# Two tiles' transposes and two long warm-up matmuls ahead of the first v matmul, and row blocks 0, 1 of v of three tiles ahead of blocks 2, 3

## The chip, the cores and the metric

The kernel runs on one core of a Trainium2 chip. A core has a matrix engine (TensorE, PE in the profile; its weight loads are PEld), a vector engine (VectorE, DVE), an engine for activations and copies (ScalarE, ACT), a general one (GpSimd, POOL) and one that issues most of the DMAs (SyncE, SP). They run side by side and wait for each other by semaphores. Matmuls read from the on-chip memory SBUF and write to banks of PSUM, a second on-chip memory; ACT and DVE read these banks.

The metric is the device time of one execution in microseconds (us). The profile shows one further execution, instruction by instruction; its times count from the span's start.

## The reference

The input x has 2048 rows (tokens) of 512 numbers in bf16. It is normalized and goes through two branches, whose outputs are added to x:

```python
xn = _layernorm(x, axis=-1)                       # 2048 x 512
# branch A: linear attention, 32 heads of 16
q, k, v = split(xn @ wqkv)                        # 512 -> 3 * 512
pq, pk = q @ w_phi, k @ w_phi                     # per head, 16 x 16
phi_q = concat(softmax(pq), softmax(-pq))         # 32 features a head; phi_k alike from pk
kv = einsum("bhsf,bhsd->bhfd", phi_k, v);  z = phi_k summed over s
o  = (phi_q @ kv) / (phi_q @ z + 1e-6)
A  = o @ wo
# branch B: gated unit, 1792 wide
B  = ((xn @ w_gate) * (xn @ w_up)) @ w_down
return x + A + B
```

## The kernel before

The tokens are cut into 16 tiles of 128 and the tiles into 4 groups of 4. A matmul contracts over the 128 partitions, so each product with xn needs xn transposed (the tile xnT: four blocks of 128 features, a token per column). A product over 512 features is four matmuls, one for each block, which add up in one PSUM bank; the helper proj (L234) issues them for the blocks that it is given.

The order of the instructions on each engine is the order in which the program writes them (the manual schedule of L98). An instruction whose input is not ready holds up all that stand behind it on its engine; only weight loads may run ahead of matmuls. Waits are set by what an instruction reads and writes.

**Loads.** SP issues tile 0 of x, tile 2 of x, then wv in two halves (blocks 0, 1 and blocks 2, 3; L84 and L85), then the first columns of the gate and up weights, and so on (L82 to L95). ACT issues tiles 1 and 3 of x (L102, L103).

**The first group.** For tiles 0 to 3 the kernel does not wait for the statistics of the normalization. DVE takes the sum of a row (sum_of, L373; for tile 1 ACT does, L376) and subtracts it from 512 times the row (sub_sum, L337), which gives the tile xn. PE transposes its four blocks (lt, L205) into a PSUM bank, and ACT copies them to xnT (L206). The scale 1/deviation comes in later, when v is copied out of PSUM (first_v_out: L361 on DVE for tiles 0 and 1, L363 on ACT for tiles 2 and 3), from statistics that DVE and POOL work out beside this (stats_of, scales_of).

**v of the first group** is done by first_v (L353): tiles 0 and 1 into two banks of their own (kvbank), tiles 2 and 3 into banks of the shared pool of six (ps_s, L143), which hands out banks in turn: first to the warm-up matmuls (L304), then to the transposes of tile 0 (two banks), tile 1, and on in the order of the program.

**Warm-up matmuls** (warm_up, L306) multiply constants into a bank that nobody reads: with the second argument left out they are 512 columns wide, with 1 they are 128 wide. Seven long ones and a short one stand at the start (L311, L312).

The order of PE around the change, before: seven long warm-up matmuls and a short one; transposes of tile 0; two short warm-up matmuls; block 0 of v of tile 0; transposes of tile 1; block 1 of v of tile 0; transposes of tile 2; blocks 2, 3 of v of tile 0; v of tile 1; transposes of tile 3; v of tile 2; v of tile 3; then the first units of the gated branch.

**The rest.** A unit of the gated branch (ffn, L265) is four gate matmuls (L274), four up matmuls (L278), a copy by ACT (L281) and a product by DVE (L282) for 128 of the 1792 columns and 512 tokens. Three units come first, then the product of wk and w_phi (fold, L217, matmuls at L225), then units mixed with k features, kv sums and, for tile 4 and later, v (vproj). Tiles 4 to 15 are normalized by ACT (L192) and transposed by a DMA (L194). After the last kv sum come attention (attend, L458) and the output matmuls (fin, L284: w_down at L290, wo at L293), whose result DVE adds to x and SP stores.

Of the kernel before, what the change touches and what calls it, by code (L numbers as in the profile page):

```python
# [21 lines left out]
def kernel(  # L22
# [19 lines left out]
    DC = D // P  # L42
# [102 lines left out]
    def bank(name, dt=F32, n=TT):  # L145
        return ps_s.tile([P, n], dt, name=name, tag="s")
# [55 lines left out]
    def lt(n, lo=0, hi=DC):  # L202
        tp = bank("tp", BF16).rearrange("p (c t) -> p c t", c=DC)
        for c in range(lo, hi):
            nc.tensor.transpose(out=tp[:, c, :], in_=xns[n][:, c * P:(c + 1) * P], identity=ident[:])  # L205
        nc.scalar.copy(out=xnT[:, lo:hi, n * P:(n + 1) * P], in_=tp[:, lo:hi, :])  # L206
# [27 lines left out]
    def proj(ps, n, w, js=range(DC)):  # L234
        for j in js:
            nc.tensor.matmul(ps, lhsT=xnT[:, j, n * P:(n + 1) * P], rhs=w[:, j, :],  # L236
                             start=(j == 0), stop=(j == DC - 1))
# [68 lines left out]
    def warm_up(k, reps=DC):  # L306
        for _ in range(k):
            nc.tensor.matmul(warm[:, 0:reps * P], lhsT=ones,
                             rhs=nc.const_aps.tensor(1.0, [P, reps * P], BF16), start=True, stop=True)

    warm_up(7)  # L311
    warm_up(1, 1)  # L312

    with tc.tile_pool(name="ps_k", bufs=1, space=PSUM) as ps_k:
        kvbank = [ps_k.tile([P, TT], F32, name=f"kv{b}") for b in range(2)]
# [20 lines left out]
        def sub_sum(n, tot, lo=0, hi=D):  # L336
            nc.vector.tensor_scalar(out=xns[n][:, lo:hi], in0=xall[:, n, lo:hi], scalar1=float(D), scalar2=tot[:],  # L337
                                    op0=ALU.mult, op1=ALU.subtract)
# [14 lines left out]
        def first_v(n, js):  # L353
            if n not in vps:
                vps[n] = kvbank[n][:] if n < 2 else bank("pv")
            proj(vps[n], n, wv, js)
# [22 lines left out]
        sub_sum(1, tots[1])  # L379
        lt(0, 0, 2)  # L380
        lt(0, 2, DC)
        warm_up(2, 1)
        first_v(0, (0,))
        lt(1)
        first_v(0, (1,))
        for n in (2, 3):
            sum_of(n)
            sub_sum(n, tots[n])
        lt(2)
        first_v(0, (2, 3))  # L390
        first_v(1, range(DC))
        lt(3)
        first_v(2, range(DC))
        for n in (2, 3, 0, 1):
            stats_of(n)
            scales_of(n, float(D))
# [125 lines left out]
```

## Time and profile before

| what | value |
|---|---|
| three runs | 220.89, 221.40, 223.25 us; median 221.4 |
| the profiled execution | 221.23 us |
| its span, first to last instruction | 219.5 us |
| mean granted TensorE clock | 0.999 |
| PE busy | 214.5 us (98%), 1292 matmuls and transposes |
| DVE, ACT, POOL busy | 141.0 (64%), 89.4 (41%), 74.1 us (34%) |
| PE's waits in the first 30 us | 1.3 us for wv (L236), 0.8 us at the start |

How to read the lines that follow in this document. A row of a timeline has the start in us, the time in us, the engine, the line of the program, the operation, what it writes<-reads, its shape, the number of instructions merged into it (x4), and in brackets how long its engine was idle before it and what ended that. Matmuls overlap in the pipeline, so a row's time is longer than what it adds: the distance from one start to the next counts. A row of the chain of waits has start, time and what the time was spent on. A row of the stretches has its bounds, its length, and then for each engine the busy time and the number of instructions in the order PE, PEld, DVE, ACT, POOL, followed by the granted clock, the share of the DMA engines and GB/s. A row of a source line gives the shortest, median and longest instruction in ns and the first and last start; below it stands the time from a DMA's issue to its landing. An engine with a q (SPq) is its queue, which only issues or waits.

### The profile page before, as it was taken

The page shows a single profiled execution, that of the slowest core. Times are in us where ns is not written, and L with a number is a line of the kernel's source. Part 1 is how long each engine was busy: PE and PEld are TensorE (multiplying, and loading weights), DVE is VectorE, ACT ScalarE, POOL GpSimd, SP SyncE. Part 2 cuts the span into 40 slices and gives each one's busy share as a digit, 9 for nine tenths or more (in the row PEclk, how much of TensorE's full clock was granted, in tenths as well). Part 3 has the DMA queues.
Part 4 walks back from the last instruction along what each step waited for, and adds up shares of the span by engine and source line. Part 5 has one row for each costly group of instructions (what it writes and reads, how often), then busy time and mean ns, then how long its engine had stood idle before and what let it go on. Part 6 is the DMA issues. An engine that isn't in the chain of part 4 may idle for free.

```text
span 219.5 us, 3489 instructions
## 1 busy us (share of the span) xinstructions
PE 214.5 (98%) x1292; PEld 102.8 (47%) x1292; DVE 141.0 (64%) x239; ACT 89.4 (41%) x159; POOL 74.1 (34%) x71
## 2 busy tenths in 40 slices
PE   6999999999999999999999999999999999999994
PEld 2444445454444444444544444444444444444443
DVE  5858866886598757667499773196655645454321
ACT  5546586459665875465434222141231322100000
POOL 2540853363348463636045433033023033000000
PEclk9999999999999999999999999999999999999999
DMA  5999996102202431202018445114451431512301
GB/s 176 283 293 371 375 242 93 42 0 51 48 0 49 50 75 21 48 3 48 1 30 98 92 106 115 47 24 96 96 75 24 96 72 27 97 48 72 74 25 48
DMA packets 48529, 19.91 MB, mean 91 GB/s; under 512 B 37504, under 2 KB 48512, under 8 KB 48512
## 3 DMA queue, kind: packets, MB, share of 16 engines
q1 hardware_dynamic: 48224, 19.42, 39.8%
q10 hardware_dynamic: 288, 0.26, 0.4%
q8 instruction: 10, 0.16, 0.3%
q14 instruction: 7, 0.06, 0.1%
HBM read 8.67 MB, written 2.10 MB: 49 GB/s over the span
## 4 chain that ended last, share of the span: by engine, by line
PE 96%; DMA 2%; SPq 0%; DVE 0%; issue 0%
PE g L274 22%; PE fin L290 22%; PE u L278 22%; PE fin L293 6%; PE k L236 6%; PE q L236 6%; PE pv L236 6%; DMA wv<-in_A_wqkv_dram 2%; PE kv L330 2%; PE ab L461 2%; PE kv L236 1%; PE pq L225 1%; SPq L69 0%; PE tp L205 0%; DVE o_sb L300 0%
## 5 line engine op out<-in xcount | busy, mean ns | idle before, releaser
L274 PE MATMUL g<-xnT,wg 128*128 128x512 bf16 x224 | 57.5, 379 | 0.0
L278 PE MATMUL u<-xnT,wu 128*128 128x512 bf16 x224 | 57.5, 379 | 0.0
L282 DVE TENSOR_TENSOR hT<-u,g_sb 128x512 bf16<-128x512 f32 x56 | 37.0, 666 | 24.9 <-PE u L278 16.8
L253 POOL TENSOR_TENSOR phiq<-e,rsum 128x1024 bf16<-128x1024 f32 x16 | 30.9, 1933 | 63.5 <-DVE rsum L251 56.0
L281 ACT CAST g_sb<-g 128x512 bf16<-128x512 f32 x56 | 32.8, 587 | 47.1 <-PE g L274 46.9
L249 DVE TENSOR_REDUCE sums<-e 128x64 f32<-128x1024 f32 x32 | 38.9, 1216 | 20.1 <-ACT e L246 20.1
L290 PE MATMUL fin<-wd,hT 128*128 128x512 bf16 (+2 forms) x238 | 51.1, 366 | 0.0
L253 POOL TENSOR_TENSOR phik<-e,rsum 128x1024 bf16<-128x1024 f32 x16 | 30.9, 1932 | 40.6 <-DVE rsum L251 38.5
L278 PEld LDWEIGHTS <-wu 128*128 128x128 bf16 x224 | 21.9, 98 | 26.4
L290 PEld LDWEIGHTS <-hT 128*128 128x128 bf16 x238 | 22.4, 98 | 24.8
L274 PEld LDWEIGHTS <-wg 128*128 128x128 bf16 x224 | 21.1, 98 | 24.0
L236 PEld LDWEIGHTS <-xnT 128*128 128x128 bf16 x192 | 17.4, 97 | 18.4 <-ACT xnT L206 0.9
L300 DVE TENSOR_TENSOR o_sb<-fin,xall 128x512 bf16<-128x512 f32 (+2 forms) x13 | 8.5, 650 | 20.5 <-PE fin L293 20.5
L251 DVE RECIPROCAL rsum<-sums 128x64 f32<-128x64 f32 x32 | 17.7, 553 | 3.1
L293 PE MATMUL fin<-wo,oT 128*128 128x512 bf16 (+2 forms) x68 | 16.6, 366 | 0.0
L236 PE MATMUL k<-W1k,xnT 128*128 128x512 bf16 x64 | 16.4, 379 | 0.0
L236 PE MATMUL q<-W1q,xnT 128*128 128x512 bf16 x64 | 16.4, 378 | 0.0
L245 ACT ACTIVATE e<-q 128x512 f32<-128x512 f32 x12 | 7.2, 597 | 22.2 <-PE q L236 22.2
L236 PE MATMUL pv<-wv,xnT 128*128 128x512 bf16 x56 | 14.2, 379 | 0.0
L474 DVE TENSOR_TENSOR otok<-ab,rden 128x512 bf16<-128x512 f32 x16 | 11.1, 692 | 0.6
L322 ACT CAST vt<-pv 128x512 bf16<-128x512 f32 x12 | 7.0, 587 | 10.0 <-PE pv L236 10.0
L153 DVE BATCH_NORM_STATS2 stats<-xall 128x6 f32<-128x512 bf16 x16 | 10.6, 665 | 0.0
(61 smaller groups left out, 130.4 us busy)
## 6 DMA issues: line engine op xcount, KB each, us to landing
out_dram<-o_sb SPq DMA_DIRECT2D x15, 128.0 KB, 2.0
wd<-in_B_w_down_dram SPq DMA_DIRECT2D x1, 1792.0 KB, 15.6
xall<-in_A_x_dram SPq DMA_DIRECT2D x1, 1024.0 KB, 11.6
wg<-in_B_w_gate_dram SPq DMA_DIRECT2D x1, 640.0 KB, 8.6
wu<-in_B_w_up_dram SPq DMA_DIRECT2D x1, 640.0 KB, 9.8
wv<-in_A_wqkv_dram SPq DMA_DIRECT2D x2, 256.0 KB, 4.4
xall<-in_A_x_dram SPq DMA_DIRECT2D x1, 512.0 KB, 4.2
wg<-in_B_w_gate_dram SPq DMA_DIRECT2D x1, 512.0 KB, 5.4
```

The lines of the kernel that those rows point to most:

```text
L153: nc.vector.bn_stats(out=stats[:], in_=xall[:, n, :])
L236: nc.tensor.matmul(ps, lhsT=xnT[:, j, n * P:(n + 1) * P], rhs=w[:, j, :], start=(j == 0), stop=(j == DC - 1))
L249: nc.vector.tensor_reduce(out=sums[:], in_=ev, axis=AX.X, op=ALU.add)
L251: nc.vector.reciprocal(out=rsum[:].rearrange("p a b -> p (a b)"), in_=sums[:])
L253: nc.gpsimd.tensor_tensor(out=phi[:].rearrange("p g (x f) -> p (g x) f", f=DH), in0=ev, in1=rsum[:].to_broadcast((P, 2 * H, DH)), op=ALU.mult)
L274: nc.tensor.matmul(gps, lhsT=wg[:, c, f * P:(f + 1) * P], rhs=xnT[:, c, T * TT:(T + 1) * TT], start=(c == 0), stop=(c == DC - 1))
L278: nc.tensor.matmul(ups, lhsT=wu[:, c, f * P:(f + 1) * P], rhs=xnT[:, c, T * TT:(T + 1) * TT], start=(c == 0), stop=(c == DC - 1))
L281: nc.scalar.copy(out=g_sb[:], in_=gps)
L282: nc.vector.tensor_tensor(out=hTs[T][:, f, :], in0=ups, in1=g_sb[:], op=ALU.mult)
L290: nc.tensor.matmul(ps, lhsT=hTs[T][:, f, t4 * P:(t4 + 1) * P], rhs=wd[:, f, lo:lo + w], start=(f == 0), stop=False)
L293: nc.tensor.matmul(ps, lhsT=oTs[n][:, c, :], rhs=wo[:, c, lo:lo + w], start=False, stop=(c == DC - 1))
L474: nc.vector.tensor_tensor(out=o_tok[:].rearrange("p (b h d) -> p b h d", b=2, d=DH), in0=abv[:, :, :, 0:DH], in1=rden[:].to_broadcast((P, ...
```

## The change

The three edits are in the order of the program, so of PE alone; ACT, DVE, POOL and SP have the same instructions in the same order.

```diff
     warm_up(7)
-    warm_up(1, 1)
+    warm_up(3, 1)
...
         lt(0, 0, 2)
         lt(0, 2, DC)
-        warm_up(2, 1)
-        first_v(0, (0,))
         lt(1)
-        first_v(0, (1,))
+        warm_up(2)
         for n in (2, 3):
             sum_of(n)
             sub_sum(n, tots[n])
         lt(2)
+        for n in range(3):
+            first_v(n, (0, 1))
+        lt(3)
         first_v(0, (2, 3))
-        first_v(1, range(DC))
-        lt(3)
-        first_v(2, range(DC))
+        first_v(1, (2, 3))
+        first_v(2, (2, 3))
         for n in (2, 3, 0, 1):
             stats_of(n)
             scales_of(n, float(D))
```

The order of PE after it: seven long warm-up matmuls and three short ones; transposes of tiles 0 and 1; two long warm-up matmuls; transposes of tile 2; blocks 0, 1 of v of tiles 0, 1 and 2; transposes of tile 3; blocks 2, 3 of v of tiles 0, 1 and 2; v of tile 3; then the gated branch as before. v of tile 2 is begun before the transposes of tile 3, so it takes the fifth bank after the warm-up's in the shared pool, and these transposes take the warm-up's. PE has two matmuls more: two short warm-up matmuls at the start; two short ones further on have become long. All that is computed stays the same.

## The prediction

> **What bounds the kernel now.** I read the page first (busy shares, the chain that ended last), then the busy time of each engine by stretches, then the chain of waits for the first 17 us, and last the rows of single engines around the start of the v matmuls.
>
> ```profile
> PE   6999999999999999999999999999999999999994
> PEclk9999999999999999999999999999999999999999
> PE 96%; DMA 2%; SPq 0%; DVE 0%; issue 0%
> ```
>
> The chain is TensorE (PE) for 96% and a DMA for 2%. The next rows give, for each stretch, its length and then the busy time of PE.
>
> ```profile
> 3.87:5.97 2.10, 0.76 (x8) 0.44 (x7) 2.06 (x6) 0.81 (x4) 0.00 (x0) 1.00 0.84 256
> 5.97:10.10 4.13, 4.12 (x29) 2.10 (x29) 3.54 (x10) 2.26 (x4) 2.27 (x6) 1.00 1.20 305
> 10.10:50.00 39.90, 39.90 (x278) 19.17 (x277) 30.72 (x50) 24.29 (x44) 18.55 (x27) 1.00 0.77 198
> 50.00:100.00 50.00, 50.00 (x288) 23.74 (x286) 35.49 (x52) 33.23 (x59) 25.16 (x17) 1.00 0.22 38
> 150.00:200.00 50.00, 50.00 (x281) 23.59 (x280) 27.43 (x48) 10.20 (x18) 9.66 (x5) 1.00 0.35 70
> ```
>
> The reader is to see that PE is full from 5.97 us on: 4.12 of 4.13, 39.90 of 39.90, 50.00 of 50.00. Before 5.97 it has holes: only 0.76 busy in 2.10. So the kernel is a wait of 5.97 us and then one unbroken row of PE work. It gets shorter only if work leaves that row or the row starts earlier.
>
> ```profile
> 1.71 4.23 DMA wv<-in_A_wqkv_dram
> 5.93 0.04 issue
> 5.97 0.38 PE kv L236
> 6.35 0.22 PE tp L205 x4
> 6.57 0.22 PE kv L236
> 6.79 0.22 PE tp L205 x4
> 7.01 1.29 PE kv L236 x6
> 8.31 0.22 PE tp L205 x4
> 8.53 1.73 PE pv L236 x8
> ```
>
> This is the chain from the load of wv to the first gate matmul. The row starts when the first half of wv lands, at 1.71 + 4.23 = 5.94. Behind that stand 16 v matmuls (0.22 each: 1.73 / 8) and three groups of four transposes (0.22 a group: tiles 1, 2, 3).
>
> ```profile
> 4.12 0.48 PE L205 MATMUL tp<-ident,xn 128*128 128x128 bf16 x4
> 4.43 0.28 PE L308 MATMUL warm<-const-bfloat16-1.0 128*128 128x128 bf16 x2
> 5.97 0.38 PE L236 MATMUL kv<-wv,xnT 128*128 128x512 bf16 x1 [1.26 <-DMA wv<-in_A_wqkv_dram]
> 10.10 1.03 PE L274 MATMUL g<-xnT,wg 128*128 128x512 bf16 x4
> ```
>
> PE idles 1.26 us ahead of the first v matmul, and the releaser is the wv load.
>
> **The change part by part.** (1) The transposes of tiles 1 and 2 (eight) move ahead of the first v matmul. In the old row they cost two chain rows of 0.22, so 0.44 us leaves the row if they fit into the idle 1.26 us. Whether they fit is a matter of when their inputs are ready, which VectorE (DVE) sets:
>
> ```profile
> 3.77 0.74 DVE L337 TENSOR_SCALAR xn<-xall,tot 128x256 bf16<-128x256 bf16 x3
> 4.43 0.68 DVE L373 TENSOR_REDUCE tot<-xall 128x1 f32<-128x512 bf16 x1
> 5.15 0.35 DVE L337 TENSOR_SCALAR xn<-xall,tot 128x512 bf16<-128x512 bf16 x1
> 6.13 0.35 DVE L337 TENSOR_SCALAR xn<-xall,tot 128x512 bf16<-128x512 bf16 x1
> 8.57 0.58 ACT L206 COPY xnT<-tp 128x512 bf16<-128x512 bf16 x1 [0.88 <-PE tp L205]
> ```
>
> Tile 1's xn is ready at 3.77 + 0.74 = 4.51, tile 2's at 5.50, tile 3's at 6.48. With about 0.05 from a DVE end to PE (5.50 to 5.55), tile 1's transposes run from 4.57 to 4.79, tile 2's from 5.55 to 5.77. Both are through before wv lands at 5.94. The cover is thin for tile 2: 0.2 us.
>
> (2) Two long warm matmuls stand between them. At full speed they take 2 x 0.22 = 0.43, from 4.79 to 5.22, in the hole in which PE would otherwise wait for tile 2's xn until 5.55. Cost nothing; with that cover gone, 0.43. In their place two short ones go away (pitch about 0.06), also out of the hole.
>
> (3) Two more short warm matmuls stand ahead of the first transposes.
>
> ```profile
> 0.82 3.21 PE L308 MATMUL warm<-const-bfloat16-1.0 128*128 128x512 bf16 x8 [0.82 <-PEq L506]
> 3.77 0.27 PE L308 MATMUL warm<-const-bfloat16-1.0 128*128 128x128 bf16 x1
> ```
>
> Seven long warm matmuls lie between 0.82 and the short one at 3.77, so they are issued 0.42 us apart, twice the later 0.22: PE is at half speed then, and a short one takes about 0.42 / 4 = 0.11. Three from 3.77 end at 4.09, just ahead of the first transposes at 4.12. I take 0; the bound is 2 x 0.11 = 0.21 later transposes of tile 0, which still lie in the hole.
>
> (4) The order of the v matmuls: blocks 0, 1 of tiles 0 to 2 (six), then tile 3's transposes, then blocks 2, 3 of the three tiles, then tile 3's v. The same 16 matmuls are issued, so the order costs nothing unless one of its waits comes late. I go through them. v of tile 1 starts at 5.97 + 0.43 = 6.40; its transposed block was copied by ScalarE (ACT, 0.58 as in the row above) by about 5.6. v of tile 2 starts at 6.84; its copy runs from about 5.97 (end of the last transpose with its pipeline) to 6.56, plus 0.05 to PE: 0.2 us of slack, the thinnest after the start itself. Tile 3's transposes start at 7.27, input ready 6.53. Blocks 2, 3 start at 7.49 and need the second half of wv:
>
> ```profile
> L75 SPq DMA_DIRECT2D wv<-in_A_wqkv_dram x2: 428/448/469, 1.7 to 2.2; - x2
> DMA to landing us min/median/max: 4.2/4.4/4.5
> 2.69 0.47 SPq L72 DMA_DIRECT2D wg<-in_B_w_gate_dram  x1
> wg<-in_B_w_gate_dram SPq DMA_DIRECT2D x1, 256.0 KB, 4.9
> ```
>
> It is issued at 2.2 and lands 4.5 later, at 6.7: slack 0.8. Tile 3's v starts at 8.79, its copy is done by 8.3. The first gate matmul would start at 5.97 + 16 x 0.216 + 0.22 = 9.65 where it starts at 10.10 now; the same sum with three groups gives 10.09, so the method holds. Its weights land at 2.69 + 4.9 = 7.6. No DMA is issued by anything that moves, and SP's queue is passed by nothing.
>
> (5) PSUM banks. Tile 2's v now takes the bank that tile 3's transposes had, and these take the warm bank. The up matmuls of the second unit, at about 12.25, then wait for ACT's eviction of tile 2's v:
>
> ```profile
> 9.50 0.69 ACT L363 ACTIVATE vt<-pv,rs 128x512 bf16<-128x512 f32 x1 [0.34 <-POOL ve L345]
> ```
>
> It ends at 10.2 even where it stands now. Free, by 2 us.
>
> (6) Everything behind comes 0.45 us earlier, and some loads don't. The transfer that comes nearest is the DMA transpose of tile 4:
>
> ```profile
> L194 SPq DMA_TRANSPOSE xnT<-xn x1: 1196/1196/1196, 27.0 to 27.0; - x1
> DMA to landing us min/median/max: 5.9/5.9/5.9
> 33.73 1.02 PE L236 MATMUL pv<-wv,xnT 128*128 128x512 bf16 x4
> ```
>
> It lands at 32.9; its first reader starts at 33.73, so it would be wanted at 33.29. Even if it does not move at all, 0.35 us stay, less some 0.2 for the weight load ahead of the matmul.
>
> Sum: -0.44, nothing given back. The profiled execution took 221.23 us for a span of 219.5, so 220.79, taken as 220.8. That execution is 0.17 below the median shown (221.4); from the median the sum is 220.96. The bounds: no more than 0.44 can go, since the start is bound by wv; and 0 if (1), (4) or (6) lose their slack.
>
> **The rivals.** *The gain is absorbed.* One of the slacks of 0.2 us (wv landing earlier than tile 2's transposes end, or tile 2's copy late) is used up, or tile 4's transfer comes later than here. Then something between 0 and 0.44 is left: 221.0 to 221.2. For it speaks that three slacks are thin; against it, that the transposes are served from engines whose rows show little wait.
>
> *Slower: tile 2's x lands late.* In the old order two v matmuls stood ahead of tile 2's transposes and its v came last; now all v matmuls queue behind them.
>
> ```profile
> 1.24 0.41 SPq L69
> DVE tot L373 <- DMA xall<-in_A_x_dram: 1.4, 1, 1.4
> DMA to landing us min/median/max: 2.2/2.6/2.9
> ```
>
> DVE waited once for x, for tile 0; tile 2's load (1.24 plus at most 2.9) was there by 4.14, 0.29 ahead of its sum. If xn of tile 2 comes at R, the new row ends at R + 0.05 + 0.22 + 3.68 = R + 3.95, the old one at R + 0.05 + 3.46 (14 matmuls and two groups). They cross where R + 3.95 = 10.10, that is R = 6.15, 0.65 later than the 5.50 here; so the load must land some 0.9 us later. From there on the change loses, up to 0.44: 221.7.
>
> *The clock comes late.* PE goes from half to full speed between 3.77 and 4.12, 3.3 us after its first warm matmul at 0.82. Suppose it does so a stretch of 3.3 us later, at 7.4. Then tile 1's transposes end at about 5.0, the long warm ones (0.42 each) at 5.83, tile 2's at 6.26, and v starts 0.29 late. Up to 7.4 PE does half of 1.14, 0.57 of the 3.68; the gate matmuls start at 10.51, 0.41 later than in this trace: 221.6. The old order would then start them at 10.8, so the change would still help against its like. Against it speaks that PE's work up to 4 us is the same and there is more behind it.
> [...]
>
> **How the numbers follow.** Sum as worked out: 0.72. Absorbed: 0.12. Tile 2's x late: 0.05. Clock late: 0.11. The likeliest is 220.8, its own range 220.2 to 221.3: the lowest run shown (220.89) less 0.44 is 220.45, and the runs' own spread is some 0.3 beside that. The other cases reach 221.7, and 221.4 + 0.4 from the median is 221.8; so 220.2 to 221.9. A measurement of this kernel can tell about 1% (2.2 us) from no change. Faster by more would need a time under 219.2, some five times what can leave the row: 0.03. Slower by more needs 223.6, two late stretches of the clock or worse: 0.05. Within 1%: 0.92.
>
> **What would show it.** Right: the first v matmul still at about 5.97 with wv as its releaser; eight transposes and two long warm matmuls ahead of it; 16 v matmuls and four transposes without a hole; the first gate matmul at 9.65; PE full behind that; a span of 219.1. Wrong: an idle row of PE ended by DVE (xn) or ACT (xnT) between 5 and 9 us, the start of v later than the landing of wv, warm matmuls at half pitch after 4.8, or a hole at 33 us ahead of tile 4's v.

## The result and the profile after

| | before | changed |
|---|---|---|
| median of 22 runs each | 221.72 us | 221.06 us |
| lowest to highest | 220.89 to 224.6 | 220.57 to 221.68 |
| profiled execution, its span | 221.23, 219.5 us | 220.88, 219.1 us |

The ratio of the runs is 0.9951, with an interval of 0.9933 to 0.997. It follows from the mean times, 222.14 and 221.06 us, without the run at 224.6, which lies over 1.5% above the fastest. The forecast time was 220.8 and its range 220.2 to 221.9. The gain by the ratio, about 1.1 us, is more than the forecast 0.44. The list of runs shows why: those of the kernel before fall in two groups. 12 of the 22 lie between 220.89 and 221.73, around 221.4; 10 lie between 222.68 and 224.6, around 223.2. The changed kernel has one group. So there are two effects: about 0.35 us between the lower group and the changed kernel (221.4 to 221.06), and an upper group that is gone.

The chain of waits of the changed kernel, from the load of x to the first gate matmul:

```profile
0.79 2.48 DMA xall<-in_A_x_dram
...
3.29 0.70 DVE tot L373
...
4.76 0.60 DVE tot L373
5.37 0.02 issue
5.39 0.37 DVE xn L337
5.76 0.05 issue
5.80 0.40 PE tp L205 x4
6.20 0.86 PE kv L236 x4
7.07 0.43 PE pv L236 x2
7.50 0.22 PE tp L205 x4
7.72 0.86 PE kv L236 x4
8.58 1.29 PE pv L236 x6
9.88 0.86 PE g L274 x4
```

Where the load of wv stood at the head of the chain stands now the load of x, the sums on DVE and xn of tile 2. Behind that are 16 v matmuls and one group of transposes, no longer three. PE's timeline:

```profile
4.36 0.86 PE L205 MATMUL tp<-ident,xn 128*128 128x128 bf16 x8
5.05 0.60 PE L308 MATMUL warm<-const-bfloat16-1.0 128*128 128x512 bf16 x2
5.80 0.40 PE L205 MATMUL tp<-ident,xn 128*128 128x128 bf16 x4 [0.15 <-DVE xn L337]
6.04 1.03 PE L236 MATMUL kv<-wv,xnT 128*128 128x512 bf16 x4
...
9.71 1.03 PE L274 MATMUL g<-xnT,wg 128*128 128x512 bf16 x4
```

From the first v matmul to the first gate matmul it is 9.71 - 6.04 = 3.67 us; before it was 10.10 - 5.97 = 4.13. That is 0.46 less, the two groups of transposes. The start is 0.07 later, so 0.39 is left, and the spans differ by as much (219.5 and 219.1). The stretches show that nothing of it is given back:

```profile
3.87:5.97 2.10, 1.87 (x17) 0.88 (x16) 2.03 (x7) 1.46 (x5) 0.00 (x0) 1.00 0.93 286
5.97:9.65 3.68, 3.68 (x24) 1.79 (x22) 3.54 (x9) 1.70 (x3) 1.68 (x5) 1.00 1.13 303
9.65:50.00 40.35, 40.35 (x281) 19.41 (x279) 31.24 (x53) 24.75 (x44) 19.52 (x29) 1.00 0.80 198
```

PE is busy for 1.87 of the 2.10 us in which it was busy for 0.76, and full from there on.

The granted clock stands at 1.00 in these rows, and in the rows of stretches further on, even where PE runs at half speed: the trace's record of the clock begins only when PE goes to full speed, at 4.13 us in this profile and at 3.87 in the one before. What lies ahead of that is read from the distance between matmuls: 512 columns take 0.42 to 0.43 us from one start to the next at half speed and 0.22 at full speed.

### The profile page after: what moved, and what is told of

Its sections match the earlier page's. It is cut to its first block, busy times and chain, and to the rows that moved or that the text cites. A ratio compares the mean times of both kernels' runs of the same rounds, so it can differ in the third digit from the quotient of the medians.

```text
span 219.1 us, 3493 instructions
## 1 busy us (share of the span) xinstructions
PE 215.2 (98%) x1294; PEld 103.1 (47%) x1294; DVE 140.9 (64%) x239; ACT 89.4 (41%) x159; POOL 74.1 (34%) x71
## 4 chain that ended last, share of the span: by engine, by line
PE 96%; DVE 1%; DMA 1%; issue 0%
PE g L274 22%; PE fin L290 22%; PE u L278 22%; PE fin L293 6%; PE k L236 6%; PE q L236 6%; PE pv L236 6%; PE ab L461 2%; PE kv L330 2%; DMA xall<-in_A_x_dram 1%; PE kv L236 1%; DVE tot L373 1%; PE pq L225 1%; DVE xn L337 0%; PE tp L205 0%
```

## The experiments

The theory after the result: PE starts at half speed, and the moment at which it goes to full speed varies from one execution to the next. In the upper group it comes only after the v matmuls have begun, because PE does too little in the hole ahead of them; the change fills the hole. The first rival: the order of the transposes alone does it, the warm-up matmuls nothing. The second: the upper group is made by loads that land late. The experiments were made in three series, each with runs of the kernel before beside it. These fell in the two groups again: 21 of 35, 17 of 29 and 14 of 23 at 222.58 or above, the others at 221.91 or below.

### The warm-up matmuls alone

```diff
-    warm_up(1, 1)
+    warm_up(3, 1)
...
-        warm_up(2, 1)
+        warm_up(2)
         first_v(0, (0,))
```

> The kernel before with the change's warm-up matmuls alone (three short ones at the start, two long ones instead of two short ones in the hole), its order of v and transposes kept. Clock theory: the runs of before fall in two groups, near 221.4 and near 223.2, because in some executions PE is still at half speed behind the hole; the longer warm-ups fill it, so the upper group goes and all runs lie near 221.4 (220.9 to 221.8), the lower group does not move. Rival, the order alone did it: the warm-ups do nothing, some 45% of the runs stay near 223.2.

Measured: 221.43 us, all 12 runs from 221.05 to 221.75; ratio 0.9955 (0.9927 to 0.9983). The upper group is gone and the lower one has not moved, as the theory had it. PE's timeline:

```profile
4.32 0.61 PE L205 MATMUL tp<-ident,xn 128*128 128x128 bf16 x4
4.72 1.06 PE L308 MATMUL warm<-const-bfloat16-1.0 128*128 128x512 bf16 x2
6.39 0.38 PE L236 MATMUL kv<-wv,xnT 128*128 128x512 bf16 x1 [0.61 <-DMA wv<-in_A_wqkv_dram]
6.61 0.38 PE L205 MATMUL tp<-ident,xn 128*128 128x128 bf16 x4
...
10.52 0.81 PE L274 MATMUL g<-xnT,wg 128*128 128x512 bf16 x3
```

In this execution the two long ones still run at half speed (1.06 for two, 0.60 in the timeline of the changed kernel), and the first v matmul behind them is at full speed (the next instruction starts 0.22 later). Full speed came while PE stood in the hole (the record begins at 6.10 us).

### The order alone

```diff
-    warm_up(3, 1)
+    warm_up(1, 1)
...
         lt(1)
-        warm_up(2)
+        warm_up(2, 1)
```

(against the changed kernel)

> The changed kernel with the warm-up matmuls of before (one short one at the start, two short ones in the hole). Clock theory: the order is worth 0.4 us in every execution, so the lower group lies near 221.0, but an upper group near 222.8 comes back in a good part of the runs. Rival, the order alone did it: all runs near 221.0 as with the whole change.

Measured: 220.92 us, all 12 runs from 220.67 to 221.19; ratio 0.9932 (0.9904 to 0.9961). The half on the lower group held; the upper group did not come back, so here the rival was right and the theory as put fell. Both halves of the change clear the upper group, each by itself, in 12 runs each. What they share is more work of PE in the hole: eight transposes in the one, 0.85 us of long matmuls at half speed in the other. This was made the theory: the amount of work decides, whatever it is.

### Less work at the start

```diff
-    warm_up(7)
+    warm_up(4)
```

(against the kernel before)

> The kernel before with four long warm-up matmuls at the start instead of seven, so that PE is idle for about 1.3 us more ahead of the transposes of tile 0. Clock theory: PE comes to full speed later, so most or all runs are in the upper group, 222.7 to 224, and the profile shows v matmuls 0.43 us apart. Rival, the upper group is made by late loads: the share near 223.2 stays at about 45%, and the profile shows v matmuls 0.22 us apart behind a later landing of wv.

Measured: 223.01 us, 12 runs from 222.15 to 224.57; ratio 1.0033 (1.0 to 1.0066). None is in the lower group; nine lie from 222.68 up, in the range of the upper group, and three (222.15, 222.16, 222.56) just below it. The profiled execution shows the half speed at the v matmuls:

```profile
5.86 0.58 PE L236 MATMUL kv<-wv,xnT 128*128 128x512 bf16 x1 [0.74 <-DMA wv<-in_A_wqkv_dram]
6.24 0.63 PE L205 MATMUL tp<-ident,xn 128*128 128x128 bf16 x4
6.67 0.63 PE L236 MATMUL kv<-wv,xnT 128*128 128x512 bf16 x1
7.09 0.63 PE L205 MATMUL tp<-ident,xn 128*128 128x128 bf16 x4
7.52 2.30 PE L236 MATMUL kv<-wv,xnT 128*128 128x512 bf16 x6
9.65 0.39 PE L205 MATMUL tp<-ident,xn 128*128 128x128 bf16 x4
```

wv landed in time (start at 5.86), but a v matmul takes 0.42 up to the next instruction and four transposes 0.43, where it was 0.22 for each. The last group, at 9.65, is at full speed (0.23 to the next start, at 9.88). Late loads don't make this execution slow.

### The v matmuls tile by tile

```diff
-        for n in range(3):
-            first_v(n, (0, 1))
-        lt(3)
-        first_v(0, (2, 3))
-        first_v(1, (2, 3))
-        first_v(2, (2, 3))
+        first_v(0, range(DC))
+        first_v(1, range(DC))
+        lt(3)
+        first_v(2, range(DC))
```

(against the changed kernel)

> The changed kernel with v of tiles 0, 1 and 2 whole, one tile after the other (tile 3's transposes ahead of tile 2's v), transposes and warm-ups as changed. Theory: blocks 2, 3 of tile 0 are then wanted at about 6.45 and their half of wv lands at 6.5 to 6.7, so 0.1 to 0.3 us is given back: 221.2 to 221.4 against 221.06. Rival, the order of the blocks is worth nothing: 221.06, within 0.1.

Measured: 221.19 us, 11 of the 12 runs from 221.03 to 221.65, one at 222.24; ratio 0.9952 (0.9922 to 0.9982). The 0.13 us above the changed kernel, whose runs are of another series, is at the lower end of what the theory had, and little beside the spread of the runs. The profile has the wait that it named:

```profile
5.87 0.59 PE L236 MATMUL kv<-wv,xnT 128*128 128x512 bf16 x2
6.66 1.45 PE L236 MATMUL kv<-wv,xnT 128*128 128x512 bf16 x6 [0.20 <-DMA wv<-in_A_wqkv_dram]
```

From start to start the first two v matmuls take 0.79 (6.66 less 5.87) where they would take 0.43, so the wait costs the row 0.36 in this execution. Once the transposes are out of the row, blocks 2, 3 come too early for their half of wv; the order by blocks covers that.

### A profile of the upper group

The kernel before was run three times more for a profile.

> The kernel before once more, for a profile. Of its runs so far some 60% lie near 223.15 and the rest near 221.4. Clock theory: a profiled execution of the upper group shows v matmuls 0.43 us apart from about 6 to about 9.4 us, then 0.22, and a first gate matmul near 11.85 where it stood at 10.10; the load of wv lands near 5.9 as in the lower group. Rival, late loads: the v matmuls are 0.22 apart and start 1.75 us later. An execution of the lower group tells nothing new.

> The kernel before, for a profile of its upper group (near 223.15), which the first try did not meet. Clock theory: v matmuls 0.43 us apart up to a release between 8.8 and 10.1 us, the load of wv as in the lower group, the first gate matmul 1.5 to 2.1 us later than 10.10. Rival, late loads: v matmuls 0.22 apart from a start near 7.7.

> As the run ahead of it, a further try for a profile of the upper group: by the clock theory half pitch of the v matmuls up to a release between 8.8 and 10.1 us; by the rival full pitch from a late start.

Measured: 221.51, 220.75 and 223.48 us. The first two are of the lower group; the third is what was sought. Its chain of waits:

```profile
1.70 5.10 DMA wv<-in_A_wqkv_dram
6.80 0.04 issue
6.84 0.58 PE kv L236
7.43 0.43 PE tp L205 x4
7.86 0.43 PE kv L236
8.28 0.43 PE tp L205 x4
8.71 1.84 PE kv L236 x6
10.55 0.22 PE tp L205 x4
10.77 1.73 PE pv L236 x8
```

Its weight loads around the change of speed:

```profile
8.93 0.15 PEld L236 LDWEIGHTS <-xnT 128*128 128x128 bf16 x1 [0.28 <-issue]
9.36 0.15 PEld L236 LDWEIGHTS <-xnT 128*128 128x128 bf16 x1 [0.28 <-issue]
9.74 0.31 PEld L236 LDWEIGHTS <-xnT 128*128 128x128 bf16 x2 [0.23 <-issue]
```

Up to 9.36 a v matmul takes 0.43 us, from 9.74 on 0.22. The first gate matmul starts at 12.34, 2.24 later than at 10.10 in the profile of the lower group. Both theories have a share: wv landed at 6.80 in place of 5.94, which is 0.87 of it; from 6.84 to about 9.7 PE does half of 2.86, which is 1.43 (sum 2.30). The third profile of the lower group, with wv at 5.45, took 220.75.

In the fourteen profiled executions of this study the start of the record of full speed and the group go together. In eleven it starts between 3.71 and 6.10 us, and they took 220.67 to 221.64 us. In three it starts between 9.21 and 9.68 (less work at the start, only transposes in the hole, and the one above), and they took 222.66 to 223.48. The landing of wv does not part them: 5.45 to 6.6 us in the eleven; 5.8, 6.3 and 6.8 in the three. So the landing moves a run within its group, and the clock makes the groups.

The upper group holds a second kind of run, though. Of its 52 runs of the kernel before in the three series, ten have a mean granted clock of 0.992; no run of the lower group is under 0.998. 0.8% of 221.5 us is 1.8 us, which half speed loses in some 3.5 us. By this estimate full speed came early in these runs and went away again for a stretch. No profile shows such an execution, so this part of the upper group stays argued.

### Only transposes in the hole

```diff
         lt(1)
-        warm_up(2, 1)
```

(against the kernel with the order alone)

> The changed order with the short warm-up matmul at the start as before and none between the transposes: only transposes of tiles 0 to 2 stand in the hole. If transposes count as activity for the clock: one group, 220.7 to 221.2, as with the two short ones in the hole (220.92). If they do not: PE has hardly any counted work between 4 and 6 us, and half or more of the runs lie in an upper group near 222.6.

Measured: 220.98 us; 7 of 12 runs from 220.6 to 221.06, 5 from 222.53 to 222.9; ratio 0.9958 (0.9924 to 0.9993). Neither expectation: the upper group is there, in 5 of 12. The profiled execution is of the upper group:

```profile
4.46 1.07 PE L205 MATMUL tp<-ident,xn 128*128 128x128 bf16 x8 [0.38 <-DVE xn L337]
5.90 0.61 PE L205 MATMUL tp<-ident,xn 128*128 128x128 bf16 x4 [0.38 <-DVE xn L337]
6.31 1.91 PE L236 MATMUL kv<-wv,xnT 128*128 128x512 bf16 x4
8.01 1.06 PE L236 MATMUL pv<-wv,xnT 128*128 128x512 bf16 x2
...
9.29 1.11 PE L236 MATMUL kv<-wv,xnT 128*128 128x512 bf16 x4
...
11.53 1.03 PE L274 MATMUL g<-xnT,wg 128*128 128x512 bf16 x4
```

Four v matmuls take 1.70 (8.01 less 6.31) in place of 0.86. The kernel with the order alone has two short warm-up matmuls more, 0.2 us of work at half speed, and none of its 12 runs is in the upper group (2 of 36 over the three kernels with the two short ones, see below).

### One long warm-up matmul in the hole

```diff
-        warm_up(2, 1)
+        warm_up(1)
         first_v(0, (0,))
```

(against the kernel before)

> The kernel before with one long warm-up matmul in the hole in place of the two short ones (0.43 us of work at half speed in place of 0.21). If a share of activity decides: more work in the hole means a smaller upper group than before's 60%, but not none as with two long ones: 10 to 50% near 223.15, the rest near 221.4. Rival, any long matmul is enough: one group near 221.4.

Measured: 221.79 us; 7 of 12 from 220.76 to 221.97, 5 from 223.11 to 223.48; ratio 0.9996 (0.9958 to 1.0033). As the theory by amount had it: fewer than before's 60%, not none, though 12 runs do not tell 5 of 12 from 17 of 29 for sure.

### The sum of tile 2 on ACT

```diff
+        nc.scalar.activation(out=junk[:], in_=xall[:, 2, :], func=AF.Identity, accum_out=tots[2][:])
...
         for n in (2, 3):
-            sum_of(n)
+            if n > 2:
+                sum_of(n)
             sub_sum(n, tots[n])
```

(against the kernel with the order alone)

> The changed order with the warm-ups of before, and the row sum of tile 2 on ACT in place of DVE. Theory: in the changed order the start of the v matmuls is set by tile 2's xn (DVE) and no longer by the load of wv; with the sum on ACT xn is ready about 0.25 us earlier and wv binds again, so 0.1 to 0.25 us less than the 220.92 without it. Rival: wv lands late enough anyway, or ACT's copies come too late: 220.9 to 221.1.

Measured: 220.97 us, 11 of 12 from 220.76 to 221.31, one at 222.88; ratio 0.9945 (0.9915 to 0.9974). No gain. The rival's time held, but for a reason that it did not name: ACT has to wait for tile 2's x, so xn comes later and not earlier:

```profile
4.58 0.63 ACT L377 ACTIVATE junk<-xall 128x512 bf16<-128x512 bf16 x1 [0.42 <-DMA xall<-in_A_x_dram]
5.33 0.35 DVE L337 TENSOR_SCALAR xn<-xall,tot 128x512 bf16<-128x512 bf16 x1 [0.70 <-ACT junk L377]
```

xn is ready at 5.68, against 5.51 in the profile of the kernel with the order alone, where DVE makes the sum (subtraction from 5.15, 0.36 long).

### The two warm-ups of the change, each cut back

```diff
-        warm_up(2)
+        warm_up(2, 1)
```

(against the changed kernel, the long ones in the hole short)

> The changed kernel with the two short warm-up matmuls of before in the hole in place of the two long ones; the three short ones at the start stay. Theory: in executions in which PE is still at half speed the two long ones take 0.85 us and push tile 2's transposes and the first v matmul behind the landing of wv, up to 0.3 us; with short ones this goes: 220.9 (against 221.06 with the long ones), at most one run in twelve in an upper group near 222.7. Rival, the long ones cost nothing: 221.05.

Measured: 221.03 us, 11 of 12 from 220.72 to 221.44, one at 223.78; ratio 0.9958 (0.992 to 0.9997).

```diff
-    warm_up(3, 1)
+    warm_up(1, 1)
```

(against the changed kernel, one short one at the start)

> The changed kernel with one short warm-up matmul at the start in place of three; the two long ones in the hole stay. Theory: the three short ones end ahead of the first transposes and cost nothing, so 221.05 as with the whole change, one group. Rival, they push tile 0's transposes: 220.9.

Measured: 221.16 us, all from 220.94 to 221.56; ratio 0.9947 (0.9918 to 0.9976). Whether the long ones in the hole cost anything stays open. The two kernels are of one series: the one with short ones is 0.13 faster, about what the theory had, but the runs overlap widely. A comparison with the 221.06 of the change settles nothing, since it is of another series: in this one the lower group of the kernel before lies near 221.1 (nine runs) and not near 221.4.

That the long ones buy margin is not shown either. With two short ones in the hole (three kernels: the order alone, the sum on ACT, this one) 2 of 36 runs were in the upper group, one of them with a granted clock of 0.992; with two long ones in the hole and the whole changed order none of 34 (the change's 22 and the last kernel's 12). That can be chance. No version tried is clearly faster than the change; the order alone lies 0.14 lower, in another series.

### How much work is enough

The record of full speed is 215.04 us long in eleven profiles and 211.63 in the three in which it begins late, so it is shorter by 3.41 us. The rows below have PE's busy time in stretches of that length, in four profiles. Full speed came at the end of the first three (kernel before, second of the three profiles, where the record begins at 5.41; warm-ups alone, 6.10; kernel before, upper group, 9.68):

```profile
2.00:5.41 3.41, 2.90 (x12) 1.09 (x10) 1.85 (x5) 1.38 (x6) 0.37 (x1) 1.00 0.91 286
```

```profile
2.69:6.10 3.41, 3.06 (x13) 1.17 (x11) 2.78 (x7) 1.37 (x4) 0.00 (x0) 1.00 1.01 314
```

```profile
6.27:9.68 3.41, 2.83 (x13) 1.55 (x13) 3.25 (x9) 1.17 (x2) 1.73 (x5) 1.00 1.05 280
```

and not at the end of these, which lie a stretch ahead of the late starts at 9.44 and 9.68 (only transposes in the hole; kernel before, upper group):

```profile
2.62:6.03 3.41, 2.65 (x15) 1.07 (x14) 2.57 (x7) 1.83 (x5) 0.00 (x0) 1.00 0.91 265
```

```profile
2.85:6.26 3.41, 2.05 (x10) 0.89 (x9) 2.94 (x7) 1.37 (x4) 0.00 (x0) 1.00 0.90 280
```

In all fourteen profiles the stretch at whose end full speed came holds 2.83 us of work or more. The stretch ahead of it, where full speed came late, holds 2.65, 2.05 and, with less work at the start, 1.2. That there is one bound between 2.65 and 2.83, and that where such a stretch begins is left to chance, is the author's estimate from these profiles and from the shares of the two groups; no run set where a stretch begins.

## Why the prediction was right, and where it was not

- *Eight transposes leave the row: 0.44.* Right. The row from the first v to the first gate matmul went from 4.13 to 3.67, and the kernel with the order alone has its lower group where the sum put it (220.92; 221.4 less 0.44 is 220.96).
- *The start stays at the landing of wv.* Wrong in its name, nearly right in size. In the profile after, wv landed at 5.75, and v started at 6.04 behind tile 2's transposes, which waited for DVE. The thin cover of 0.2 us was named; x landed 0.24 later here (tile 0's sum starts at 3.29, before at 3.05), and that used it up. This is the absorbed rival in a mild form: 0.39 in place of 0.44. Two signs that the prediction gave for being wrong are there: an idle row of PE ended by xn (0.15 us at 5.80), and a start of v later than the landing of wv.
- *Warm-up matmuls cost nothing.* Right for the profile after: behind the long ones PE still waits 0.15 us for tile 2's xn. For executions in which the long ones run at half speed it stays open; the two kernels that cut them back leave room for 0.1 us or so.
- *The order of the blocks costs nothing.* Right, and it is worth something, since blocks 2, 3 would else wait for wv: 0.36 us in one profile, 0.13 between the medians of two series.
- *Banks, tile 4's DMA transpose.* Right: PE's only waits in the profile after are at the start and the 0.15 for tile 2's xn.
- *The base of the sum.* This is the step that failed: the sum was made against one profiled execution and a median of three runs, as if the kernel before had one time. One of the three (223.25) was of another kind. The clock rival had the mechanism, the half speed of the v matmuls, but too small a price: an execution of the old order with full speed at 7.4 was to start the gate matmuls at 10.8, 0.7 late; in the upper group's profile full speed comes at 9.7 and they start at 12.34, 2.24 late (0.87 of it from the landing of wv). The 7.4 was an assumption, and no profile shows it: the record of full speed begins between 3.71 and 6.10 us or between 9.21 and 9.68. And the rival was taken as a chance of 0.11 for the new kernel, and what it meant for the old one, over 1.7 us in half of its runs, was not put into the forecast. So the time came out within the range, and the gain was 1.1 us by the ratio in place of 0.44. It was luck that the one profile shown was of the lower group, on which the sum for the new kernel holds.

## What to carry to other kernels

Look at each single run before a sum is made: two groups in the times of the kernel before mean that one profile shows only one of them, and the larger part of a gain can be that one group goes. A wait at the start of a kernel is worth filling, first with real work (transposes that stand in the row behind it), then with a few dummy matmuls if PE is not yet sure to run at full speed; here the longer dummy matmuls alone left none of 12 runs in the upper group, and the transposes with the two short ones of before none of 12 either, but the transposes with none left 5 of 12. When work moves ahead of a load, ask what else it waits for: the load of x and DVE's sums became the head of the chain.

## What the runs showed of the hardware that was not expected

- The moment of full speed varied far more than one profile let see: in the profiles of this study the record of the full clock begins between 3.71 and 9.68 us with the same first 3 us of work (one kernel with less work at the start apart).
- Eight transposes in the hole, with the two short warm-up matmuls of before, left none of 12 runs in the upper group, as the longer warm-up matmuls did. The kernel before and the one with the order alone have the same warm-up matmuls; the eight transposes in the hole are the difference there (the order of the v matmuls behind it changes too), and the upper group went from about 60% (21 of 35) to none of 12. The profile lists these transposes as matmuls, issued 0.11 us apart at half speed and 0.055 at full speed (four in 0.43 and in 0.22).
- The first half of wv, issued at 1.70 to 1.71 us in both, landed at 5.94 in one profile of the kernel before and at 6.80 in another.
